# Twenty-four of the first gates' weights converted during attention in place of sixteen, with w2's conversions and three loads at other places of the order

## The chip, the core and the metric

The kernel runs on one core of one Trainium2 chip. The metric is the time of one execution on the device, in microseconds; the median of three runs of the kernel before is 1388.04 us (1387.42 to 1390.29).

## What is computed

Four batches of 12-head attention (448 positions, 64 dimensions a head) whose scores and whose probabilities are each mixed across the heads by a 12x12 matrix; then a gated feed-forward layer and a second one, over 1792 tokens of width 768:

```python
scores = einsum('bhij,hg->bgij', q @ k.T / 8, w_pre)
attn = einsum('bhij,hg->bgij', softmax(scores), w_post)
x = (attn @ v).transpose(0, 2, 1, 3).reshape(1792, 768)
x = (sigmoid(x @ w_gate) * (x @ w_val)) @ w_out          # first: 768 -> 1536 -> 768
h = x @ w_in2
out = (h * sigmoid(1.702 * h)) @ w_out2                  # second: 768 -> 2048 -> 768
```

The five feed-forward weights come as 64-bit floats. Each has to be turned into a 32-bit float on the chip, and this is the "conversion" that the change moves.

## The kernel before, in words

**Products.** Every product is made of 32-bit values split into a high and a low part, in three matmuls. A weight tile (384 columns of 128 rows) becomes a pair of parts by `high` on ScalarE (ACT, line 913) and `low` on VectorE (DVE, line 919).

**A conversion** (`convert`, lines 786 to 799) takes a piece of 384 KB from its input to a 32-bit tile of 192 KB and stores it in device memory (`kept`). It is one load on SyncE's queue (SP), two ACT instructions (lines 791, 792), three DVE instructions (lines 794, 795, 797), and a store on SP's queue (line 799). There are 136 pieces: 48 of the first layer's gate and value weights (four for each of twelve gate blocks f), 24 of its output weight, 32 of w2's input weight and 32 of w2's output weight. Sixteen of the first 48 (`self.pre`, line 633) are converted while attention runs, through one buffer `pf` for the load and two buffers `pc` for the result (`prepare`, lines 820 to 845). The other 120 are converted in the feed-forward part through buffers `ws` and `wc`.

**Attention** (lines 85 to 523) takes 180 groups of ten query rows for all heads. A group's way is: transfer of the scores (SP), split in high and low (ACT, then GpSimd or DVE, line 278), mix before (TensorE, line 285), maximum (DVE, line 292), exponential (ACT, line 299), normalizing (DVE, ACT), mix after (TensorE, line 330), copy out; and for each of 16 units of up to 12 groups the product with v (line 349). The order on each engine is made by a planner (`Work`, lines 21 to 77): each piece has a due time and costs per engine, and the planner always takes the piece that can start first, the earlier due one among equals. A conversion's pieces are due at its entry of `TIMES` (us, line 548), and its load may not be planned before that. On the chip each engine and each queue then works its own list strictly in order.

**The feed-forward part** is written out in program order. `take` (line 944) hands TensorE the next split weight, `ahead` (line 951) has four or five more weights' steps put out beyond it, `split` (line 931) puts out one step of the list `units`: pieces used at once ("f"), pieces converted and stored alone, and pieces that are made from stored ones ("o", "p", "s"). The list is written in lines 632 to 659; where a conversion stands in it sets beside which product its instructions run. In order:

- Token half t = 0, first four gate blocks ("direct", f = 0 to 3), plain products with 16 weights, each converted on the spot. Beside them `widen` (line 1232) builds sums of the activations for the faster form of product that follows: a load of x (four transfers of 224 KB) for each of three chunks, four DVE sums a chunk (line 1190), and splits. `pump` (line 1122) hands out these steps at each half product, `later_work` sets the rate.
- Four pairs of gate blocks (f = 4, 6, 8, 10), 14 products each in the faster form, whose weights are loaded back from `kept` by `lift` (line 886, four transfers of 384 KB a pair), when `allowed` and the pair's last conversion permit it. Beside the pairs run 5, 6, 5 and 3 conversions.
- The output product with 24 weights converted on the spot (line 1353); 13 conversions of w2's pieces stand between them, from the third weight on. Blocks 0 and 1 of the gates were stored, and are split again at the start (lines 1356 to 1360, so lines 983 and 985), just before they are used.
- t = 1: six pairs with three conversions each, then the output product, now with weights loaded back in twelve pairs (`kept_pair`, line 593), and two or three conversions after each, from the first on.
- Then the second layer for t = 1 and for t = 0.

Of the kernel before, what the change touches and what calls it, by code (L numbers as in the profile page):

```python
# [526 lines left out]
class Ffn:  # L527
# [16 lines left out]
    EARLY = 4  # L544
    SPILL = 2
    DIRECT = 4
    PRE = 16
    TIMES = (85, 94, 121, 124, 145, 150, 166, 190, 232, 238, 276, 292, 319, 331, 371, 382)
    NST = 5
    DOWN = 2.0 ** -112  # L550
    MOST = 122879.9921875 * DOWN
# [2 lines left out]
    def __init__(self, ctx, tc, xd, yd, gd, kept, sums2, w_gate, w_val, w_out, w2_in, w2_out, out):  # L554
# [9 lines left out]
        KG, KD, K1, K2 = self.KG, self.KD, self.K1, self.K2  # L564
# [4 lines left out]
        o1 = len(self.pieces)  # L569
# [16 lines left out]
        def whole(i, used=True):  # L586
            u = len(self.units)
            self.units.append(("f", len(self.items), i))
            self.items.append(("f", i, u + 1))
            if used:  # L590
                self.used.append(u)

        def kept_pair(i):
            u = len(self.units)
            self.used += [u, u + 1]
            self.units += [("p", len(self.items), x) for x in range(2)]
            self.items.append(("k", i, u + 3))
# [13 lines left out]
        rest = [*range(o3, len(self.pieces)), *range(o2, o3)]  # L611
        D = self.DIRECT
# [3 lines left out]
        def convert(*pieces):  # L616
            for i in pieces:
                where[i] = len(self.units)
                whole(i, False)

        def kept_own(j, others):
            loads = [[4 * (j + f) + 2 * g for f in range(2)] for g in range(2)]
            after = max(where[i + x] for y in loads for i in y for x in range(2)) + 2
            self.groups.append((loads, after))
            n = len(self.groups) - 1
            spread = [len(others) * min(x, 8) // 8 for x in range(15)]
            for x, (p, g) in enumerate((p, g) for p in self.ORDER for g in range(2)):
                self.used.append(len(self.units))
                self.units.append(("o", (n, g), p))
                convert(*others[spread[x]:spread[x + 1]])  # L630

        early = [*range(4 * D, o1)]
        self.pre = [early.pop(0) for _ in range(self.PRE)]
        where.update((i, -3) for i in self.pre)
        for i in range(4 * D):
            where[i] = len(self.units)
            whole(i)
            if early and False:
                convert(early.pop(0))
        for n, j in enumerate(range(D, K1, 2)):  # L640
            m = (5, 6, 5, 0)[n]
            convert_now = [early.pop(0) for _ in range(min(m, len(early)))]
            if j == K1 - 2:
                convert_now += [rest.pop(0) for _ in range(3)]
            kept_own(j, convert_now)
        assert not early
        for i in range(o1, o2):
            where[i] = len(self.units)
            whole(i)
            if i > o1 + 1 and (i - o1) % 5 in (0, 2, 4):  # L650
                convert(rest.pop(0))
        for j in range(0, K1, 2):
            kept_own(j, [rest.pop(0) for _ in range(3)])
        for i in range(o1, o2, 2):
            kept_pair(i)
            for _ in range(3 if i % 4 else 2):
                if rest:
                    convert(rest.pop(0))
        assert not rest
        self.ends = []  # L660
# [11 lines left out]
        self.steps = {}  # L672
        self.kblocks = []
        self.spare = 45
        self.allowed = 1
        self.later = []
        self.done = set()
        self.step = 0
# [141 lines left out]
    def prepare(self, work, pf, pc):  # L820

        last = []
        for n, i in enumerate(self.pre):
            t = self.TIMES[n] * 1e3
            tiles = {}
# [146 lines left out]
    def load(self, dst, src, c):  # L972
        self.nc.sync.dma_start(dst[:, 1].bitcast(F32), src[:, c, :])
# [258 lines left out]
    def widen(self):  # L1232

        A, X, KG = self.A, self.X, self.KG
        raw = {}

        def load(c):
            raw[c] = [self.form(F32) for _ in range(2)]
            for x, cc in zip(raw[c], (c, KG + c)):
                for h in range(2):  # L1240
                    self.nc.sync.dma_start(x[:, h], self.xd[h][:, cc, :])

        def sums(c):
            (x1, x3), (x2, x4) = ((x[:, 0], x[:, 1]) for x in raw[c])
            self.tt(x4, x3, x4, ALU.add)
            self.tt(x3, x1, x3, ALU.subtract)
            self.tt(x1, x4, x1, ALU.subtract)
            self.tt(x2, x2, x1, ALU.subtract)

        def parts(c, j):  # L1250
            for p, x in (((7, raw[c][0][:, 1]), (5, raw[c][1][:, 1])), ((6, raw[c][0][:, 0]), (3, raw[c][1][:, 0])))[j]:
                A[p].append(self.form())
                self.hilo(A[p][c], x)
            if j:
                self.after(1, lambda: self.give(*raw[c]))

        for c in range(KG):
            A[1].append(X[c][0])
            A[2].append(X[KG + c][0])
            A[4].append(X[KG + c][1])  # L1260
        yield lambda: load(0)
        yield lambda: load(1)
        for c in range(KG):
            yield lambda c=c: sums(c)
            yield lambda c=c: parts(c, 0)
            yield lambda c=c: (parts(c, 1), load(2) if c == 0 else None)
# [47 lines left out]
    def first(self, t):  # L1314

        K1, S, D = self.K1, self.S, self.DIRECT
        G = self.G = [[None, None] for _ in range(K1)]
        if t:
            self.later_work(self.sums_out(range(3), 3), 38)
        else:  # L1320
            self.A = {p: [] for p in self.ORDER}
            self.later_work(self.widen(), 4 * D - 7)
            self.spare = 12
        for f in range(K1):
            if t or f >= D:
                if f % 2:
                    self.spare = 0 if f < self.SPILL else 4
                    if f < K1 - 1:
                        self.allowed += 1
                    self.gates(t, f - 1, f == K1 - 1)  # L1330
                if t and f == 5:
                    self.rush()
            else:
                if f == 0:
                    pg, pv = (acc for acc, _ in self.going)
                else:
                    pg, pv = (self.banks(name, 2) for name in ("pg", "pv"))
                    for acc in (pg, pv):
                        for k, _ in enumerate(self.product(acc, self.X)):
                            if k % self.KG == self.KG - 1:  # L1340
                                self.pump()
                self.gated(t, f, pg, pv)
                if f == D - 1:
                    self.rush()
                    self.give(*(self.X[c][1] for c in range(self.KG)))
        self.flush()
        self.next = {p: [] for p in self.ORDER}
        if t:
            self.A = self.next
            self.later_work(self.sums_out(range(3, 4)), 17)  # L1350
        steps = K1 // self.KG
        act = G[self.KG:] + G[:self.KG]
        for m in range(self.KD):
            py = self.banks("py", 2)
            for k, _ in enumerate(self.product(py, act)):
                if m == 0 and k in (2 * self.KG - 2, 2 * self.KG - 1):
                    for h in range(2):
                        x = G[k - 2 * self.KG + 2][h]
                        self.part(self.nc.scalar, x, 0)
                        self.after(0, lambda x=x: self.part(self.nc.vector, x, 1))  # L1360
                if not t and k % self.KG == 0:
                    self.next_a(self.xd[2:], m * steps + k // self.KG,
                                {8 * c + x: [(c, i)] for c in range(self.KG) for i, x in enumerate((0, 4, 6))})
                if m == self.KD - 1:
                    self.give(*act[k])
                    if k == 0 and not t:
                        self.allowed, self.spare = self.allowed + 1, 0
                if k % self.KG == self.KG - 1:
                    self.pump()
            if t:  # L1370
                if m == 4:
                    self.rush()
                self.next_y(m, py)
            else:
                for h in range(2):
                    y = self.temp("y")
                    self.nc.scalar.copy(y, py[h][:, :S])
                    self.nc.sync.dma_start(self.yd[h][:, m, :], y)
        self.A = self.next
# [272 lines left out]
```

## Time and profile before

| | |
|---|---|
| median of three runs | 1388.04 us |
| the profiled execution | 1385.28 us |
| its span, first to last instruction | 1383.5 us |
| attention's last matmul (line 349) starts | 466.75 us |
| TensorE clock granted | 1.0 of full speed throughout |
| busy share: TensorE / DVE / ACT | 98% / 78% / 66% |

Times in all rows count from the span's start. PE is TensorE's matmuls, PEld its weight loads, POOL is GpSimd, SP is SyncE, whose work is issuing transfers. A busy time of TensorE is modelled from pipelined instructions: two back to back overlap, so the number of matmuls started in a stretch tells more than its busy share. "Idle before" is the time in which an engine stood still ahead of an instruction, with what ended it.

### The profile page before, as it was taken

What the parts mean: (1) busy time and instruction counts of PE and PEld (TensorE: products, weight loads), DVE (VectorE), ACT (ScalarE), POOL (GpSimd) and SP (SyncE); (2) the same over time, 40 slices, a digit from 0 to 9 for tenths busy, and PEclk for the clock granted to TensorE, in tenths of its full rate; (3) what the DMA queues carried; (4) which work ended last, traced back from release to release, by engine and by line L of the source; (5) the groups of instructions that cost most, each with busy time, mean ns of one, the idle gap of its engine ahead of it and who ended that gap; (6) DMA issues with size and microseconds to landing.
All of it is one profiled execution on the core that took longest, in us unless ns stands there. A gap on an engine that the chain in (4) does not pass through costs nothing.

```text
span 1383.5 us, 26030 instructions
## 1 busy us (share of the span) xinstructions
PE 1351.1 (98%) x8904; PEld 1232.7 (89%) x8904; DVE 1079.7 (78%) x2473; ACT 909.8 (66%) x2142; POOL 170.4 (12%) x160
## 2 busy tenths in 40 slices
PE   7999999999999999999999999999999999999999
PEld 5888888888888989898999999899999999999998
DVE  6788878878888879989879987887876679566664
ACT  5878778887888746767666666664766355566352
POOL 3444433433440000000000000000000000000000
PEclk9999999999999999999999999999999999999999
DMA  6645744743545675548997644687551587121574
GB/s 167 181 153 158 216 141 130 218 153 112 166 146 179 222 256 160 183 158 262 301 310 271 218 137 136 220 285 238 203 179 53 169 267 262 56 86 58 174 235 157
DMA packets 222084, 255.09 MB, mean 184 GB/s; under 512 B 70124, under 2 KB 209664, under 8 KB 221952
## 3 DMA queue, kind: packets, MB, share of 16 engines
q1 hardware_dynamic: 220928, 253.19, 56.9%
q8 instruction: 70, 1.15, 0.3%
q14 instruction: 62, 0.51, 0.1%
q10 hardware_dynamic: 960, 0.23, 0.1%
q0 software_dynamic: 64, 0.01, 0.0%
HBM read 159.92 MB, written 54.92 MB: 155 GB/s over the span
## 4 chain that ended last, share of the span: by engine, by line
PE 56%; DVE 2%; issue 1%; ACT 0%; DMA 0%; DVEq 0%; ACTq 0%
PE pq L1052 30%; PE po L1513 15%; PE py L997 11%; DVE wc L795 0%; DMA ws<-in_moe_w_in_dram 0%; DVE wc L797 0%; DVE w L919 0%; DVE xy L1034 0%; DVE wc L794 0%; DVE s L1190 0%; ACT xy L985 0%; DVE xy L983 0%; ACT wc L791 0%; DVE s L1061 0%; ACT ws L792 0%
## 5 line engine op out<-in xcount | busy, mean ns | idle before, releaser
L1052 PE MATMUL pq<-xy,w 128*128 128x448 f32 x2268 | 462.7, 365 | 1.4 <-DVE s L1190 1.3
L1052 PEld LDWEIGHTS pq<-xy,w 128*128 128x128 f32 x2268 | 425.0, 188 | 38.4 <-ACT w L913 1.7
L1513 PE MATMUL po<-wf,xy 128*128 128x384 f32 x1200 | 209.4, 336 | 0.0
L1513 PEld LDWEIGHTS po<-wf,xy 128*128 128x128 f32 x1200 | 209.1, 188 | 0.1
L278 POOL TENSOR_TENSOR ghl<-gt,ghl 120x448 fp32r<-120x448 f32 (+1 forms) x144 | 165.7, 1156 | 247.2 <-ACT ghl L214 189.8
L997 PE MATMUL py<-xy,w 128*128 128x448 f32 x864 | 177.8, 365 | 5.7 <-DVE xy L983 4.0
L330 PEld LDWEIGHTS pso<-w,ex 120*112 120x112 f32 (+1 forms) x1440 | 160.5, 177 | 24.8 <-ACT w L312 6.3
L997 PEld LDWEIGHTS py<-xy,w 128*128 128x128 f32 x864 | 161.8, 188 | 21.4 <-DVE xy L983 5.3
L330 PE MATMUL pso<-w,ex 120*112 120x120 f32 (+1 forms) x1440 | 173.3, 269 | 6.7 <-ACT ex L299 2.0
L285 PE MATMUL psp<-ghl,wphl 120*120 120x448 f32 x540 | 137.6, 383 | 2.0 <-ACT ex L299 0.9
L292 DVE TENSOR_REDUCE st<-psp 120x1 f32<-120x448 f32 x180 | 109.2, 613 | 23.1 <-PE psp L285 22.9
L299 ACT ACTIVATE ex<-psp,st 120x448 f32<-120x448 f32 x180 | 113.5, 634 | 9.1 <-DVE st L292 4.6
L1033 ACT CAST xy<-xy 128x384 fp32r<-128x384 f32 (+2 forms) x188 | 85.3, 478 | 42.3 <-DVE xy L1190 40.6
L1034 DVE TENSOR_TENSOR xy<-xy 128x384 fp32r<-128x384 f32 (+2 forms) x188 | 92.2, 509 | 19.8 <-ACT xy L1033 19.5
L285 PEld LDWEIGHTS psp<-ghl,wphl 120*120 120x120 f32 x540 | 89.1, 182 | 15.8 <-issue 2.4
L791 ACT ACTIVATE wc<-ws 128x384 f32<-128x384 f32 x120 | 66.3, 553 | 44.0 <-DMA ws<-in_moe_w_in_dram 20.1
L214 ACT CAST ghl<-gt 120x448 fp32r<-120x448 f32 (+1 forms) x141 | 79.2, 568 | 23.1 <-PE psp L285 17.0
L1190 DVE TENSOR_TENSOR xy<-xy 128x384 f32<-128x384 f32 (+1 forms) x148 | 81.5, 558 | 14.0 <-DMA xy<-xd 7.2
L919 DVE TENSOR_TENSOR w<-wt,w 128x384 fp32r<-128x384 f32 x104 | 56.9, 552 | 29.3 <-ACT w L913 29.2
L349 PEld LDWEIGHTS psv<-at,vt 112*64 112x64 f32 x1536 | 73.7, 137 | 5.4 <-issue 2.8
L349 PE MATMUL psv<-at,vt 112*64 112x120 f32 (+1 forms) x1536 | 77.1, 260 | 0.2
L913 ACT CAST w<-xy 128x384 fp32r<-128x384 f32 x100 | 50.0, 511 | 38.7 <-DVE xy L1190 34.3
(98 smaller groups left out, 1828.1 us busy)
## 6 DMA issues: line engine op xcount, KB each, us to landing
gt<-sc SPq DMA_DIRECT2D x172, 210.0 KB
wf<-sb SPq DMA_DIRECT2D x64, 384.0 KB
kept<-wc SPq DMA_DIRECT2D x120, 192.0 KB
xy<-kept SPq DMA_DIRECT2D x56, 384.0 KB
ws<-in_moe_w_out_dram SPq DMA_DIRECT2D x56, 384.0 KB
ws<-kept SPq DMA_DIRECT2D x44, 384.0 KB
sb<-xy SPq DMA_DIRECT2D x32, 384.0 KB
ws<-in_moe_w_in_dram SPq DMA_DIRECT2D x32, 384.0 KB
```

What stands on the lines that cost most here:

```text
L278: eng.tensor_tensor(out=t[:m, 1], in0=gt.pop(s)[:m], in1=t[:m, 0].bitcast(F32), op=ALU.subtract)
L285: nc.tensor.matmul(ps[:m, :S], wphl[:m, wp, :m], t[:m, gp], start=(i == 0), stop=(i == 2))
L292: nc.vector.tensor_reduce(out=st[:m, 0:1], in_=pre[s][:m, :S], axis=AX.X, op=ALU.max, negate=True)
L299: nc.scalar.activation(t[:m], pre.pop(s)[:m, :S], AF.Exp, bias=st[:m, 0:1], scale=1.0, accum_out=st[:m, 1:2])
L330: nc.tensor.matmul(ps[:JC, c, :, :n], e[:m, c * JC:(c + 1) * JC], w[:m, :, :n], start=True, stop=True)
L349: nc.tensor.matmul(ps[a * 64:a * 64 + 64, r, :n], vt[b][:, g, c, :], a_t[:, c, g, :n], start=(c == 0), stop=(c == NJ - 1), tile_position=( ...
L997: self.nc.tensor.matmul(acc[hb][:, :self.S], st, act[k0 + kc][hb][:, ap], start=(k0 + kc == 0 and part == 0 and ap == 0), stop=(k0 + kc == ...
L1033: self.nc.scalar.copy(dst[:, 0], src)
L1034: self.after(n, lambda: self.nc.vector.tensor_tensor(out=dst[:, 1], in0=src, in1=dst[:, 0].bitcast(F32), op=ALU.subtract))
L1052: nc.tensor.matmul(x, st, A[p][c][:, ap], start=(first and c + part + ap == 0), stop=(c == self.KG - 1 and part == 1), skip_group_check=no ...
L1190: self.nc.vector.tensor_tensor(out=dst, in0=x, in1=y, op=op)
L1513: nc.tensor.matmul(acc[:, :PW], x[:, part], w[:, wp], start=(start and part == 0 and wp == 0), stop=(stop and part == 1), skip_group_check ...
```

## The change

It converts 24 pieces during attention, all weights of f = 4 to 9, at other times; the other eight (f = 10, 11) are converted beside the pairs f = 4 and f = 6, four each, and four of w2's pieces each beside the pairs f = 8 and f = 10. In the first output product ten of w2's pieces are converted, from behind the sixth weight on, where there were thirteen from behind the third. In the second output product the conversions begin behind the third pair of weights, three a pair. `widen`'s first load is issued when its list is made, ahead of the first gate block's end, an empty step is put behind its second load, and the list is spread over ten hand-outs, where there were nine. The first `lift` is allowed at f = 2, and no longer from the start.

```diff
-    PRE = 16
-    TIMES = (85, 94, 121, 124, 145, 150, 166, 190, 232, 238, 276, 292, 319, 331, 371, 382)
+    PRE = 24
+    TIMES = (82, 83, 94, 128, 129, 145, 155, 159, 190, 195, 206, 229, 239, 264, 265, 278, 292, 303, 334, 335, 342, 356, 366, 391)
@@ the list of units
-            if early and False:
-                convert(early.pop(0))
         for n, j in enumerate(range(D, K1, 2)):
-            m = (5, 6, 5, 0)[n]
+            m = (4, 4, 0, 0)[n]
             convert_now = [early.pop(0) for _ in range(min(m, len(early)))]
-            if j == K1 - 2:
-                convert_now += [rest.pop(0) for _ in range(3)]
+            if j > 7:
+                convert_now += [rest.pop(0) for _ in range(4)]
             kept_own(j, convert_now)
@@
-            if i > o1 + 1 and (i - o1) % 5 in (0, 2, 4):
+            if i > o1 + 4 and (i - o1) % 2:
                 convert(rest.pop(0))
@@
             kept_pair(i)
-            for _ in range(3 if i % 4 else 2):
-                if rest:
+            for _ in range(3):
+                if rest and i > o1 + 3:
                     convert(rest.pop(0))
@@
-        self.allowed = 1
+        self.allowed = 0
@@ widen
-        yield lambda: load(0)
+        load(0)
         yield lambda: load(1)
+        yield lambda: None
@@ first
-            self.later_work(self.widen(), 4 * D - 7)
+            work = self.widen()
+            work = [next(work), *work]
+            self.later_work(work, 4 * D - 6)
@@
+                if f == D // 2:
+                    self.allowed += 1
```

## Rows read from the trace of the kernel before

**Rows 1.** The page: busy us, share of span, instructions of each engine.

```profile
PE 1351.1 (98%) x8904; PEld 1232.7 (89%) x8904; DVE 1079.7 (78%) x2473; ACT 909.8 (66%) x2142; POOL 170.4 (12%) x160
```

**Rows 2.** Chain that ended last: start us, us, what.

```profile
720.68 150.02 PE pq L1052 x738
...
874.21 5.81 DMA ws<-in_moe_w_in_dram
```

**Rows 3.** Windows: us, PE, PEld, DVE, ACT, POOL busy (count), clock, DMA share, GB/s.

```profile
476.00:524.00 48.00, 45.41 (x220) 40.74 (x219) 36.26 (x76) 25.06 (x52) 0.00 (x0) 1.00 0.74 243
...
550.00:577.00 27.00, 25.67 (x126) 23.31 (x125) 25.03 (x53) 18.51 (x40) 0.00 (x0) 1.00 0.59 190
...
629.00:660.00 31.00, 28.04 (x136) 25.11 (x135) 30.00 (x67) 23.39 (x51) 0.00 (x0) 1.00 0.93 301
...
660.00:720.00 60.00, 60.00 (x298) 55.53 (x297) 47.61 (x104) 37.53 (x82) 0.00 (x0) 1.00 0.94 312
...
872.00:890.00 18.00, 15.31 (x70) 12.44 (x68) 15.19 (x34) 10.67 (x24) 0.00 (x0) 1.00 0.73 228
...
890.00:966.00 76.00, 76.00 (x376) 70.41 (x377) 60.50 (x129) 41.62 (x92) 0.00 (x0) 1.00 0.86 284
```

**Rows 4.** Timeline of PE: start us, us, instruction, idle before.

```profile
505.98 3.10 PE L997 MATMUL pv<-xy,w 128*128 128x448 f32 x14 [1.28 <-DVE w L919]
...
557.38 71.97 PE L1052 MATMUL pq<-xy,w 128*128 128x448 f32 x351 [1.33 <-DVE s L1190]
...
643.88 16.41 PE L997 MATMUL py<-xy,w 128*128 128x448 f32 x78 [2.90 <-DVE xy L983]
...
884.23 2.75 PE L997 MATMUL py<-xy,w 128*128 128x448 f32 x11 [1.16 <-ACT xy L1033]
...
889.39 2.83 PE L997 MATMUL py<-xy,w 128*128 128x448 f32 x11 [1.14 <-DVE xy L983]
```

**Rows 5.** Timeline of SP, ACT and DVE at the first gates.

```profile
480.19 2.02 SPq L893 DMA_DIRECT2D xy<-kept  x4
...
483.25 2.81 SPq L1241 DMA_DIRECT2D xy<-xd  x4
...
489.70 0.55 ACT L791 ACTIVATE wc<-ws 128x384 f32<-128x384 f32 x1 [4.77 <-DMA ws<-in_moe_w_gate_dram]
...
492.02 2.61 DVE L1190 TENSOR_TENSOR xy<-xy 128x448 f32<-128x448 f32 x4 [7.23 <-DMA xy<-xd]
```

**Rows 6.** Groups by line, conversions and GpSimd: busy us, mean ns.

```profile
L795 DVE SCALAR_TENSOR_TENSOR pc<-pc,pf 128x384 uint32<-128x384 uint32 x16 | 11.6, 724 | 0.4
...
L797 DVE SCALAR_TENSOR_TENSOR pc<-pf,pc 128x384 uint32<-128x384 uint32 x16 | 11.0, 690 | 0.2
...
L794 DVE TENSOR_SCALAR pc<-pc 128x384 f32<-128x384 f32 x16 | 8.4, 526 | 2.9 <-ACT pc L791 2.9
...
L795 DVE SCALAR_TENSOR_TENSOR wc<-wc,ws 128x384 uint32<-128x384 uint32 x120 | 66.1, 551 | 0.8
...
L797 DVE SCALAR_TENSOR_TENSOR wc<-ws,wc 128x384 uint32<-128x384 uint32 x120 | 66.4, 554 | 1.8
...
L794 DVE TENSOR_SCALAR wc<-wc 128x384 f32<-128x384 f32 x120 | 42.4, 353 | 22.0 <-ACT wc L791 21.8
...
L278 POOL TENSOR_TENSOR ghl<-gt,ghl 120x448 fp32r<-120x448 f32 (+1 forms) x144 | 165.7, 1156 | 247.2 <-ACT ghl L214 189.8 <-DVE st L292 14.6 <-DVE ghl L214 8.3
```

**Rows 7.** Windows in attention, as in rows 3; the last: tile pc alone.

```profile
40.00:440.00 400.00, 391.56 (x3799) 341.50 (x3798) 326.96 (x881) 325.28 (x852) 157.56 (x137) 1.00 0.51 160
...
340.00:360.00 20.00, 20.00 (x192) 17.09 (x189) 16.62 (x40) 14.88 (x37) 6.30 (x6) 1.00 0.41 142
...
340.00:360.00 20.00, 3.41 (x6) 0.88 (x2) 1.00 0.41 142
```

**Rows 8.** Tiles pc, sc: ns min/median/max, first and last start.

```profile
L799 SPq DMA_DIRECT2D kept<-pc x16: 331/345/607, 110.3 to 409.4; - x16
...
L214 DVE COPY sc<-psq x97: 596/610/625, 10.6 to 426.3; 120x448 f32<-120x448 f32 x70, 88x448 f32<-88x448 f32 x27
```

## The prediction, made before the change was run

> **What bounds the kernel now.** I read the page first. TensorE is busy 98% of the span, DVE 78% [rows 1]; so whatever the change does to DVE, ACT or transfers counts only where TensorE stands still for it. The chain of waits comes next: in the feed-forward part it runs through TensorE for long unbroken pieces (738 matmuls in 150.02 us, 0.203 us each) and leaves it in a few short places, as where a load of w2 holds it for 5.81 us [rows 2]. The windows by stage then say what these places cost. An undisturbed stretch starts 298 matmuls in 60 us, 0.2013 us each [rows 3]. Against that:
>
> - 476 to 524 (direct gate blocks): 220 started where 238 fit; 18 x 0.2013 = 3.6 us lost.
> - 550 to 577 (pair f = 6): 126 where 27 / 0.203 = 133 fit; 1.4 us.
> - 629 to 660 (output product, t = 0): 136 where 154 fit; 3.6 us.
> - 872 to 890 (output product, t = 1): 70 where 89 fit; 3.9 us [rows 2, 3].
>
> Together 12.5 us, and the timeline of TensorE shows an idle row in each place, with a late DVE or ACT instruction as its end [rows 4]. Attention is another kind of stage: TensorE is busy 391.56 of 400 us there, while DVE has 73.0 and ACT 74.7 us idle [rows 7]. The change takes work out of the four places and puts it into that stage.
>
> **Direct blocks: widen's first load earlier, the first lift later.** Now SP issues the lift (four transfers of 384 KB) at 480.19 and only then, at 483.25, the first load of x; the DVE sums that need it stand at the head of DVE's list and wait 7.23 us, and the weights that TensorE then waits for are queued behind them [rows 4, 5]. With the load ahead of the first block's end it is issued some 5 us sooner (the 2.02 us of the lift, the wait for the gate, and a hand-out), and 1.5 MB of the lift no longer travels with it. The sums keep their hand-out, the third. So I count the 7.23 us wait as gone and with it the stalls: 3.2 of 3.6 us, between 1.28 (the longest idle row alone) and 3.6. What it passes: on SP the load now stands before the two stores of the first gate, which is 2.81 us of issue [rows 5]; they free two of seven buffers, which nobody wants for a whole gate block of about 14 us. The lift, at f = 2, puts four issues (2.02 us) before weight loads; that is a rival below. It has until the first pair at 524, some 30 us. The empty step moves the second chunk's sums back by one hand-out; I cost it and the tenth hand-out at nothing, since the splits are forced out before the first pair anyhow.
>
> **Pairs: 5, 6, 5, 3 conversions become 4, 4, 4, 4.** A conversion takes DVE 0.353 + 0.551 + 0.554 = 1.46 us [rows 6]. In pair f = 6 DVE is busy 25.03 of 27 us and the stall ends on a DVE sum [rows 3, 4]; two conversions less are 2.9 us less. I take all 1.4 us (bounds 0 and 1.4). The last pair gets one conversion more, early in the pair; DVE's idle time there covers it, and if it did not, up to 1.46 us would come back in the next item.
>
> **First output product.** DVE is busy 30.00 of 31 us, and TensorE waits 2.90 us for the low parts of the stored gate blocks, which stand in DVE's list behind the conversions [rows 3, 4]. By the new list two of w2's conversions that were ahead of them come later: 2 x 1.46 = 2.9 us. I take 2.9 of the 3.6 us (0 to 3.6). Later on ten conversions stand where thirteen did.
>
> **Second output product.** Here the list opened with w2 conversions whose loads had not landed; ACT works in order and waited for them, and the last gates' splits and the stored blocks' splits came late: idle rows of 1.16 and 1.14 us [rows 2, 4]. No conversion now stands beside the first two pairs of weights, five fewer. I take 3.7 of 3.9 us (0 to 3.9). The price lies behind it: three conversions a pair of weights where 2.5 were. From 890 to 966 the DMA share is 0.86 [rows 3]; it rises to at most 0.86 x 3 / 2.5 = 1.03, less as far as it is other traffic. I take nothing for it, since 660 to 720 ran at 0.94 and lost none [rows 3]; the upper bound is 0.03 x 76 = 2.3 us.
>
> **Attention: eight more conversions.** In this stretch the three DVE instructions take 0.526 + 0.724 + 0.690 = 1.94 us, a third more than the same instructions in the feed-forward part; what is there and not here is GpSimd, 1.156 us an instruction [rows 6]. Eight are 15.5 us of DVE's 73.0 idle; ACT's two instructions and the transfers (share 0.51) have more room [rows 7]. The cost for TensorE is not in any row. Below: nothing, as the stretch from 340 to 360 holds the work of two conversions (six DVE instructions, 3.41 us) and TensorE was busy all of it [rows 7]. Above: all 15.5 us. In between: TensorE's 8.4 idle us of the 400 come from late work on engines that are 82% busy; if they grow as DVE's ratio of busy to idle time does, from 327/73 to 342.5/57.5, that is a factor of 1.33, 2.8 us more. Nearest are the window without loss and this estimate; I take 2.0. A gain is not excluded either, as all pieces get another order: as much the other way, 2.8. On SP each new load waits for the one buffer `pf`, with the score transfers of later groups behind it; these are planned four groups ahead, which covers a few us.
>
> By the Trainium skill (SBUF — State Buffer, "Who interferes with whom") a DVE instruction with two SBUF inputs, or in a two-port mode, and a GpSimd instruction that reads SBUF hold one shared port by turns, and the later one is blocked until the other has ended. The longer durations agree with it. By that rule alone the added 24 DVE instructions could each wait out one of GpSimd's, 24 x 1.156 = 27.7 us of DVE, where the rows of the present conversions make it 8 x 0.48 = 3.9; this estimate is no end of my range.
>
> **Sum.** 3.2 + 1.4 + 2.9 + 3.7 = 11.2 us gained, 2.0 paid: 9.2 us. The profiled execution took 1385.28 us (span 1383.5), 2.8 under the median of three, 1388.04; so 1376.1 for a like execution and **1378.8** for the median. A measurement of this kernel can tell about 0.2%, 2.8 us, from no change.
>
> **Rivals.**
>
> *DVE in attention becomes the bound (slower).* The place is DVE's in-order list: each conversion holds a maximum or a copy behind it, whose group's whole chain waits. If all 1.94 us of each is paid, +15.5 - 11.2 = +4.3: 1392.3. It decides from 1.4 us a conversion on. For it: those stretched durations [rows 6]. Against: the unhurt window and 73 us of idle DVE [rows 7]. The skill's port rule above is its mechanism. Chance 0.09.
>
> *DMA fills up in the second output product.* The start is freed, but three conversions a pair of weights outrun the transfers: 2.3 us back, 9.2 - 2.3 = 6.9: 1381.1; if late loads also bring the 3.7 us back, 1384.8. For it the bound of 1.03, against it the 0.94 without loss. Chance 0.17.
>
> *The lift is now in the weights' way.* Its 1.5 MB at f = 2 delay weight loads as they did at 480, where ACT waited 4.77 us for one [rows 5]. Then the direct blocks stall as before: 9.2 - 3.2 = 6.0, 1382.0. Against it: weights are made four ahead, some 14 us. Chance 0.10.
>
> *The conversions end too late: no change.* The last store of a conversion came at 409.4, 27.4 us behind its time of 382, and the feed-forward part may open only after both it and the last scores at 426.3 [rows 8]. With 391 it is 418.4. With 24 in one buffer the lag may grow; past 35 us every further us delays the first weights, and 9 us more would take the gain: 1388. Chance 0.08.
>
> **How the numbers follow.** The forecast's own case has 0.56. Its own range: from all 12.5 with no cost in attention (1375.5), or 2.8 gained there (1372.7), to the low bound of the direct blocks and the last pair's 1.46 paid, 9.2 - 1.92 - 1.46 = 5.8 (1382.2). The range of 8 in 10 goes on to the middle cases and stops short of the slow one: 1372.5 to 1387. Faster by over 0.2% (under 1385.3) holds nearly all of the first case and of the two middle ones, a little of the late end: 0.78. Within 0.2%: the late end, and the edges of the others: 0.13. Slower (above 1390.8): the DVE case, 0.09.
>
> **What would show it.** Right: the idle row of the sums on DVE (7.23) gone; 236 or more matmuls in the 48 us of the direct blocks; no idle row on TensorE in pair f = 6; the row of 2.90 under 1; none over 0.5 at the second output product; attention's last product with v starting within 3 us of 466.75. Wrong: that start later by 10 or more; conversions in attention far over 1.94 us on DVE; a DMA share near 1 with idle rows of TensorE behind 890; or the four stalls still there, each behind another instruction.

## The result, and the profile after

| | before | after |
|---|---|---|
| median (lowest to highest) of 6 runs | 1388.80 us (1386.96 to 1390.60) | 1377.09 us (1375.46 to 1377.82) |
| profiled execution / its span | 1385.28 / 1383.5 us | 1377.82 / 1375.9 us |
| attention's last matmul starts | 466.75 us | 470.48 us |
| from there to the end of the span | 916.7 us | 905.4 us |

The ratio is 0.9914, with a 95% interval of 0.9903 to 0.9925: 11.7 us faster by the medians. The compared profiles differ by 7.5 us only; the last section says where the rest comes from.

The windows of after by stage, which answer to [rows 3, 7]: us, PE, PEld, DVE, ACT, POOL busy (count), granted clock, DMA share, GB/s.

```profile
476.00:524.00 48.00, 48.00 (x238) 44.48 (x238) 39.77 (x82) 29.88 (x62) 0.00 (x0) 1.00 0.86 291
550.00:577.00 27.00, 27.00 (x134) 24.82 (x133) 23.73 (x50) 17.78 (x38) 0.00 (x0) 1.00 0.49 156
627.00:658.00 31.00, 29.86 (x146) 27.04 (x146) 29.69 (x65) 22.90 (x50) 0.00 (x0) 1.00 0.89 281
658.00:718.00 60.00, 60.00 (x298) 55.52 (x297) 47.41 (x104) 36.31 (x78) 0.00 (x0) 1.00 0.91 304
869.00:887.00 18.00, 18.00 (x90) 16.64 (x90) 15.94 (x36) 12.65 (x27) 0.00 (x0) 1.00 0.73 243
887.00:958.00 71.00, 71.00 (x353) 65.74 (x352) 56.16 (x121) 39.95 (x87) 0.00 (x0) 1.00 0.86 283
...
40.00:440.00 400.00, 391.48 (x3788) 338.56 (x3789) 332.82 (x890) 334.88 (x869) 161.76 (x139) 1.00 0.56 171
```

Three of the four places run as fast as undisturbed stretches: 238 matmuls in 48 us where 220 stood, 134 where 126, 90 where 70. The first output product has 146 where 136 were. The DMA share behind the second product's start is 0.86 and nothing is lost there.

The timeline of TensorE in after says the same (start us, us, instruction, idle before). A row without an idle entry is one unbroken run.

```profile
516.96 7.46 PE L995 MATMUL pv<-xy,w 128*128 128x448 f32 x36
524.26 103.14 PE L1050 MATMUL pq<-xy,w 128*128 128x448 f32 x504
627.24 11.52 PE L995 MATMUL py<-xy,w 128*128 128x448 f32 x56
639.83 76.80 PE L995 MATMUL py<-xy,w 128*128 128x448 f32 x376 [1.08 <-DVE xy L981]
...
774.23 96.80 PE L1050 MATMUL pq<-xy,w 128*128 128x448 f32 x475 [0.44 <-DVE w L917]
870.88 87.68 PE L995 MATMUL py<-xy,w 128*128 128x448 f32 x432
```

Of the stalls of [rows 4], 1.28, 1.33, 1.16 and 1.14 are gone, 2.90 is 1.08, and a small new one of 0.44 stands among the six pairs of t = 1. On SP and DVE at the first gates of after, the load of x (line 1239) stands ahead of the stores of the gates, and the sums (line 1188) no longer wait:

```profile
480.36 2.87 SPq L1239 DMA_DIRECT2D xy<-xd  x4
483.33 0.85 SPq L1024 DMA_DIRECT2D gd<-sg  x2
...
488.27 2.59 DVE L1188 TENSOR_TENSOR xy<-xy 128x448 f32<-128x448 f32 x4
```

The row of 7.23 us idle [rows 5] has no successor.

### The profile page after: what moved, and what is told of

Read it like the earlier page. It is cut to its first block, busy times and chain, and to the rows that moved or that the text cites. A ratio compares the mean times of both kernels' runs of the same rounds, so it can differ in the third digit from the quotient of the medians.

```text
span 1375.9 us, 26033 instructions
## 1 busy us (share of the span) xinstructions
PE 1350.6 (98%) x8904; PEld 1231.9 (90%) x8904; DVE 1076.8 (78%) x2465; ACT 915.1 (67%) x2149; POOL 174.2 (13%) x161
## 4 chain that ended last, share of the span: by engine, by line
PE 71%; DVE 7%; DMA 3%; ACT 2%; issue 2%; POOL 0%; SPq 0%; DVEq 0%; ACTq 0%; POOLq 0%
PE pq L1050 29%; PE po L1516 15%; PE py L995 12%; PE pso L330 4%; PE psv L349 3%; PE psp L285 2%; PE pg L995 2%; PE pv L995 2%; PE psq L245 1%; DMA sb<-xy 1%; DVE st L292 1%; DMA xy<-kept 1%; DMA gt<-sc 1%; ACT ex L299 1%; DVE w L917 1%
## 5 line engine op out<-in xcount | busy, mean ns | idle before, releaser
L278 POOL TENSOR_TENSOR ghl<-gt,ghl 120x448 fp32r<-120x448 f32 (+1 forms) x145 | 169.5, 1175 | 245.9 <-ACT ghl L214 193.7
L285 PE MATMUL psp<-ghl,wphl 120*120 120x448 f32 x540 | 141.8, 386 | 4.9 <-POOL ghl L278 1.7
L789 ACT ACTIVATE wc<-ws 128x384 f32<-128x384 f32 x112 | 62.0, 554 | 39.3 <-DMA ws<-in_moe_w_in_dram 20.6
L214 ACT CAST ghl<-gt 120x448 fp32r<-120x448 f32 (+1 forms) x137 | 76.3, 569 | 16.5 <-PE psp L285 9.8
L312 ACT ACTIVATE w<-wpost,st 120x120 f32<-120x120 f32 x180 | 69.9, 399 | 9.5 <-DVE st L309 8.0
```

The costliest lines, as they stand in the source:

```text
L278: eng.tensor_tensor(out=t[:m, 1], in0=gt.pop(s)[:m], in1=t[:m, 0].bitcast(F32), op=ALU.subtract)
L285: nc.tensor.matmul(ps[:m, :S], wphl[:m, wp, :m], t[:m, gp], start=(i == 0), stop=(i == 2))
```

## The experiments

Stages tell more than totals here. A stage runs from the start of its first matmul to the start of the next stage's first, read from TensorE's timeline. Attention's entry is the start of its last matmul with v; the 24 matmuls of the first gate block that run before it are not counted to the direct blocks. All in us, one profiled execution each; the stages not shown differ by about 1 at most, but for one start of the second layer, of which the text tells.

| kernel | attention | direct | 4 pairs | 1st output | 6 pairs | 2nd output |
|---|---|---|---|---|---|---|
| before | 466.75 | 57.32 | 104.94 | 91.34 | 153.68 | 91.77 |
| before_again | 466.46 | 56.76 | 105.00 | 92.90 | 155.34 | 94.60 |
| after | 470.48 | 53.61 | 102.97 | 89.24 | 154.40 | 87.51 |
| after_again | 468.86 | 53.61 | 102.90 | 89.24 | 153.68 | 87.51 |
| att_only | 470.74 | 57.39 | 103.22 | 92.97 | 153.92 | 92.46 |
| no_dve_in_attention | 467.23 | 53.61 | 102.98 | 89.24 | 153.68 | 87.52 |
| times_shifted | 468.43 | 53.61 | 102.91 | 89.24 | 153.68 | 87.51 |
| loads_only | 464.91 | 53.61 | 104.41 | 92.42 | 153.52 | 94.24 |
| load_first_lift_as_before | 468.26 | 53.61 | 104.58 | 92.86 | 153.52 | 93.04 |
| second_output_only | 466.26 | 57.36 | 104.95 | 92.53 | 153.94 | 89.09 |
| first_output_later | 468.62 | 57.46 | 104.95 | 89.24 | 154.72 | 92.71 |
| second_output_28 | 466.08 | 56.77 | 104.97 | 92.93 | 153.99 | 87.48 |
| sixteen_in_attention | 467.69 | 53.61 | 106.09 | 89.18 | 155.90 | 87.52 |
| parts_first | 469.89 | 53.61 | 102.91 | 87.56 | 154.18 | 87.52 |

The theory was the prediction's: four separate stalls go, attention pays about 2 us. Its rivals were that attention pays more through DVE, that the lift gets in the way, and that one part does most of the work.

### The kernel before once more (before_again, no edit)

> The kernel before, unchanged, for a second profile. If attention's length varies from run to run, as the medians suggest (11.7 us between them, where the two profiles lie 7.5 us apart), the last matmul with v starts somewhere from 466 to 471 us and the part behind it again takes 916.7 us, within 0.5. If attention is as fixed as the rest, it starts at 466.75 within 0.5, and the profiled execution takes 1385 us.

Its profiled execution took 1390.71 us (span 1388.9); 15 timed runs of before beside it have a median of 1388.83. The two profiles of one program differ by 5.4 us, nearly all of it from the first output product to the second: 92.90, 155.34 and 94.60 us in place of 91.34, 153.68 and 91.77. So neither of the two expected cases came: attention was as long as before, but the part behind it took 922.4 us where it took 916.7. In the first output product the idle row is as long as before and only the granted clock differs; in the second the clock differs and the idle rows are 0.9 us longer; in the six pairs three small idle rows, 0.9 us together, are new at a full clock. The last section has the clock.

### Attention's part alone

```diff
 (on before)
-    PRE = 16
+    PRE = 24
-    TIMES = (85, 94, ...
+    TIMES = (82, 83, 94, ...
```

> The kernel before with PRE and TIMES of the change alone: eight conversions more in attention, which leaves 5, 3, 0 and 3 beside the four pairs. Theory (attention covers them): the part behind the last matmul with v falls by the 2.0 us that the pairs gave, from 916.7 to some 914.7; attention takes 0 to 4 us more than that of the kernel before, so the time is between 2 us faster and 2 us slower. Rival (DVE's list in attention becomes the path): 8 x 1.94 = 15.5 us more in attention, 13.5 us slower in all.

1391.05 us against 1388.83 of before: ratio 1.0016 (1.0005 to 1.0027). Attention's end moves from some 466.9 us (mean of the eight profiles with the old order, 464.9 to 468.6) to 470.74; with after and after_again (468.86) the mean of the new order is 470.0. So the eight conversions cost attention about 3.1 us. Profiles of one order differ by as much among themselves, so this mean is an estimate, uncertain by 1 to 2 us. What their going buys is the pair stall alone (103.22). The part behind attention takes 918.4 us and not the expected 914.7: both stalls in the output products stay, and the clock falls behind each, as in before_again (922.4) and unlike the first profile of before (916.7). By itself this part loses.

### Attention's DVE work left out

```diff
 (on after, prepare)
-            for j, engines in enumerate((dict(ACT=(920, 1140)), dict(DVE=(270, 360)), ...
+            for j, engines in ((0, dict(ACT=(920, 1140))), (4, dict(SP=(700, 3000)))):
```

> The changed kernel with the three DVE instructions of all 24 conversions in attention left out (loads, ACT's two and the stores stay; the weights stored are not the weights), 24 x 1.96 = 47 us of DVE. Theory (hidden): attention is at most 3 us shorter, the rest unchanged, time within 0.25% of the changed kernel's. Rival (DVE's list is the path there, a third of the work or more on it): 16 us or more faster.

1373.26 us, 0.9885 (0.9863 to 0.9907) of before; that is 3.8 us under after, 0.28% where at most 0.25% was expected. Loads, ACT's step and stores of all 24 stay. Taking away all 47 us of DVE work (24 x 1.957, from the groups below) moves attention's end from 470.0 to 467.2, 2.8 us, by one profile of this kernel; the planner also orders the rest anew when these pieces are gone. The groups of after in attention by line (busy us, mean ns of one | idle before), which answer to [rows 6], and one of them by tile (ns min/median/max):

```profile
L278 POOL TENSOR_TENSOR ghl<-gt,ghl 120x448 fp32r<-120x448 f32 (+1 forms) x145 | 169.5, 1175 | 245.9 <-ACT ghl L214 193.7 <-PE psq L245 13.5 <-PE pso L330 12.7
...
L793 DVE SCALAR_TENSOR_TENSOR pc<-pc,pf 128x384 uint32<-128x384 uint32 x24 | 18.6, 775 | 0.8
L795 DVE SCALAR_TENSOR_TENSOR pc<-pf,pc 128x384 uint32<-128x384 uint32 x24 | 16.0, 666 | 0.2
...
L792 DVE TENSOR_SCALAR pc<-pc 128x384 f32<-128x384 f32 x24 | 12.4, 515 | 5.1 <-ACT pc L789 5.1
...
L793 DVE SCALAR_TENSOR_TENSOR pc<-pc,pf x24: 540/558/1466, 95.7 to 420.9; 128x384 uint32<-128x384 uint32 x24
```

The three DVE instructions have 775 + 666 + 515 = 1.96 us, where the sixteen had 1.94. Half of them run as fast as in the feed-forward part (median 558 ns); a few of up to 1466 make the mean. DVE is not attention's bound: by these profiles some 6% of the conversions' DVE work reaches TensorE (an estimate, 2.8 of 47 us).

### The conversions due at other moments

```diff
 (on after)
-    TIMES = (82, 83, 94, 128, ...  356, 366, 391)
+    TIMES = (86, 87, 98, 132, ...  360, 370, 387)
```

> The changed kernel with every entry of TIMES 4 us later (the last 4 earlier): the same work in another order of attention. If attention's length depends on the order that the planner happens to find, it moves by 1 us or more, either way; if on the work alone, it stays within 0.5 us of the changed kernel's (by the medians). The part behind it takes 905.5 us within 0.5.

1376.43 us (1375.36 to 1378.91), which can't be told from after's 1377.09. Attention ends at 468.43, where the other moments gave 468.86 to 470.74. Of the two expected cases neither is shown: the shift is no larger than the 1.6 us between two profiles of the unchanged kernel. The last store's moment sets nothing either. By tiles in after, the last store of a conversion starts 8 us before the last copy of the scores [rows 8]:

```profile
L797 SPq DMA_DIRECT2D kept<-pc x24: 330/344/489, 97.7 to 422.1; - x24
...
L214 DVE COPY sc<-psq x100: 594/609/625, 10.1 to 430.1; 120x448 f32<-120x448 f32 x75, 88x448 f32<-88x448 f32 x25
```

### The loads alone, and without the later lift

```diff
 (on before)
-        self.allowed = 1
+        self.allowed = 0
...
-        yield lambda: load(0)
+        load(0)
         yield lambda: load(1)
+        yield lambda: None
...
-            self.later_work(self.widen(), 4 * D - 7)
+            work = self.widen()
+            work = [next(work), *work]
+            self.later_work(work, 4 * D - 6)
...
+                if f == D // 2:
+                    self.allowed += 1
```

The second kernel leaves out the two edits of `allowed`.

> The kernel before with the edits of the loads alone (widen's first load ahead, the empty step, ten hand-outs, the first lift at f = 2). Theory: the wait of DVE for x was what delayed the weights, so the direct blocks take 53.6 us where they took 57.3 and nothing else changes: 3.7 us less behind attention. Rival (the lift's transfers delay the weights anyway): 55 us or more, with TensorE waiting behind loads of the gates' weights.

> As loads_only, but the first lift stays allowed from the start, so its four transfers follow widen's first load on the queue, ahead of the weights. If the early load alone cures the stall, the direct blocks take 53.6 us as there; if the 1.5 MB of the lift still hold up x or the weights, 54.5 to 57.

1383.77 us, 0.9964 (0.9951 to 0.9977), and 1385.27 us, 0.9981 (0.9965 to 0.9997), against 1388.17 of before. The direct blocks take 53.61 us in both. The earlier load of x alone does it; the lift's place changes nothing there, and its 1.5 MB at f = 2 harm nothing. In the profiles all of the difference between the two lies in attention (464.91 and 468.26), which the lift doesn't touch; behind it the second is even 1.0 us shorter (915.2 for 916.2). A part of the difference is the clock: in the second kernel's profile TensorE stands idle for 2.23 us at 24.5, and from 28 to 32 the granted clock is 0.62, where it is 1.00 in loads_only. The other stalls stay, as the timeline of TensorE in loads_only shows:

```profile
551.36 71.91 PE L1052 MATMUL pq<-xy,w 128*128 128x448 f32 x351 [1.33 <-DVE s L1190]
...
637.79 77.89 PE L997 MATMUL py<-xy,w 128*128 128x448 f32 x376 [2.88 <-DVE xy L983]
...
879.93 2.75 PE L997 MATMUL py<-xy,w 128*128 128x448 f32 x11 [2.01 <-ACT xy L1033]
...
885.10 78.34 PE L997 MATMUL py<-xy,w 128*128 128x448 f32 x376 [1.16 <-DVE xy L983]
```

### The second output product's list alone, with 30 conversions and with 28

```diff
 (on before)
-            for _ in range(3 if i % 4 else 2):
-                if rest:
+            for _ in range(3):
+                if rest and i > o1 + 3:
 (second_output_28 also)
-                convert_now += [rest.pop(0) for _ in range(3)]
+                convert_now += [rest.pop(0) for _ in range(5)]
```

> The kernel before with the rule of the second output product alone: no conversion beside the first two pairs of weights, three beside each later one. Theory: the first weights no longer wait behind conversions whose loads are late, so that product takes 87.5 us where it took 91.8, 4.3 us less, nothing else. Rival (the transfers fill up): 88.5 us or more, with the DMA share near 1 and TensorE idle at some later weight.

> The kernel before with the rule of the second output product (as in second_output_only) and two of w2's conversions more beside the last pair of the first half, five for three, so that 28 and not 30 are left for the second product. Theory (two conversions too many at its end were what stopped the second layer's start): the second output product takes 87.5 to 89 us, the first stretch of the second layer 102.6 where second_output_only had 106.2; time 3 to 5 us below the kernel before. Rival (three a pair of weights fill the transfers whatever their number): that stretch stays over 104.5, no gain.

The first: 1388.52 us, 1.0000 (0.9987 to 1.0013). Its product runs without a stall (87.64 us for 432 matmuls), but the stalls come back behind it. TensorE's timeline in second_output_only, and one row of DVE's:

```profile
875.22 87.64 PE L997 MATMUL py<-xy,w 128*128 128x448 f32 x432
964.31 0.67 PE L1052 MATMUL pq<-xy,w 128*128 128x448 f32 x2 [1.45 <-ACT w L913]
966.11 4.94 PE L1052 MATMUL pq<-xy,w 128*128 128x448 f32 x23 [1.12 <-DVE w L919]
971.77 19.39 PE L1052 MATMUL pq<-xy,w 128*128 128x448 f32 x94 [0.73 <-DVE xy L1034]
991.97 8.28 PE L1052 MATMUL pq<-xy,w 128*128 128x448 f32 x39 [0.81 <-DVE w L919]
...
960.17 0.56 DVE L855 TENSOR_TENSOR wt<-ws 128x384 f32<-128x384 f32 x1 [4.03 <-DMA ws<-kept]
```

With the rule alone 30 pieces are left for ten pairs of weights, three behind every pair to the last, and the loads of the second layer's first weights come late: DVE stood still 4.03 us for one. The idle rows make 4.1 us, and the second layer's first stage takes 106.2 us where it took 102.6 in before. The transfers are behind there: their share is 0.90 from 880 to 940, and they still run from 960 to 965 (0.85), when the product ends. That is the mechanism of the prediction's rival of full transfers, felt one stage later than the prediction put it.

With two pieces given to the pair f = 10 before, 28 are left, as in after, and the time is 1382.29 us, 0.9954 (0.9939 to 0.9969), 6.3 us under the 1388.59 beside it. The second output product takes 87.48 us and the second layer's first stage 103.10; the transfers are done by 960 (a share of 0.00 from 960 to 965), before the product ends at 962.4. So this part of the change is worth its price only with the two pieces moved elsewhere.

### The first output product's list alone

```diff
 (on before)
-            if i > o1 + 1 and (i - o1) % 5 in (0, 2, 4):
+            if i > o1 + 4 and (i - o1) % 3:
```

> The kernel before with the same thirteen conversions of w2 in the first output product, but none before the sixth weight. Theory (two conversions of DVE stood ahead of the stored blocks' low parts): that product takes 88.9 to 89.5 us where it took 91.3; about 1 us of the stall stays. Rival (DVE is late there from the pairs on): 90.5 or more.

The number of conversions in it stays at 13. The stage does as expected: 89.24 us, as in after. The total doesn't show it: 1387.54 us, 1.0001 (0.9988 to 1.0014), with ten runs from 1385.6 to 1393.4. The product is 3.7 us shorter than in before_again, and the medians show 0.6. In the profile attention ended at 468.62 and the six pairs took 154.72, both above most others; whether the later conversions cause that or whether it is spread isn't settled.

### All but the eight conversions in attention

```diff
 (on after)
-    PRE = 24
+    PRE = 16
-    TIMES = (82, 83, 94, ...
+    TIMES = (85, 94, ...
-            m = (4, 4, 0, 0)[n]
+            m = (5, 6, 5, 0)[n]
-            if j > 7:
-                convert_now += [rest.pop(0) for _ in range(4)]
+            if j > 9:
+                convert_now += [rest.pop(0) for _ in range(6)]
-            if i > o1 + 4 and (i - o1) % 2:
+            if i > o1 + 4 and ((i - o1) % 2 or i - o1 in (10, 16)):
```

> The changed kernel with sixteen conversions in attention as before, and the eight others back beside the pairs: 5, 6, 5 and 6 conversions there, twelve (from behind the sixth weight on) in the first output product, 28 in the second; loads as changed. Theory: attention is 3 to 4 us shorter than in the changed kernel, the pairs take 1.5 to 3 us more and the first output product 1 to 3 us more; in all from 1 us faster to 2 us slower than the changed kernel, 0.9905 to 0.993 of the kernel before. Rival (the eight must leave the pairs for the rest to work): stalls return in the pairs and the output products, 0.996 or more.

1377.58 us, 0.9923 (0.9908 to 0.9938), beside 1376.31 of after_again. All four runs of it (from 1376.66) lie above all four of after_again (to 1376.53), but by so little that a difference is suggested and not shown. Twenty-two conversions beside the pairs cost two stalls there (timeline of TensorE):

```profile
554.14 51.82 PE L1050 MATMUL pq<-xy,w 128*128 128x448 f32 x252 [1.33 <-DVE s L1188]
607.32 20.41 PE L1050 MATMUL pq<-xy,w 128*128 128x448 f32 x99 [1.36 <-DVE s L1188]
```

That is 106.09 us for 102.90 in the pairs, and two idle rows of 0.77 and 0.75 stand in the six pairs (155.90 for 153.68); attention gives back 1.2 to 2.8. Here the profile shows more than the median: the profiled execution, 1380.19 us, is the slowest of the four. Against what was expected, the first output product is no longer than in after (89.18), and attention gains less than 3 to 4 us. The eight conversions in attention are a trade of nearly equal terms, worth 1.3 us by the medians. Most of the gain of the change comes from its other parts.

### The stored blocks split first

```diff
 (on after, with the TIMES of times_shifted)
-                if m == 0 and k in (2 * self.KG - 2, 2 * self.KG - 1):
+                if m == 0 and k < 2:
                     for h in range(2):
-                        x = G[k - 2 * self.KG + 2][h]
+                        x = G[k][h]
```

> The changed kernel with the shifted TIMES and with the stored gate blocks split at the first two steps of the output product, ahead of the conversions that delayed them in DVE's list. Theory: the stall of 1.1 us that is left there goes, the first output product takes 87.5 us where it took 89.2, and attention ends as in times_shifted, 2 us before the changed kernel's; time 1373 to 1375, 0.989 to 0.990 of the kernel before. Rival (another weight is late instead, as conversions now wait behind the splits): 89 us there, no gain over times_shifted.

1373.76 us (1373.56 to 1375.01), 0.9894 (0.9880 to 0.9909) of before, 2.6 under after_again (1375.43 to 1376.53) on the same chip. Of this the stage accounts for 1.7 us, 87.56 for 89.24; the rest isn't placed, for attention ended at 469.89, and not where it did in times_shifted. The low parts of the two stored blocks (line 981) are put out with the first two of the product's twelve blocks, no longer with the fifth and sixth, and so stand ahead of some of the weights' conversions in DVE's list; they are used at the tenth and eleventh. The first output product in its timeline is one row:

```profile
626.57 87.72 PE L995 MATMUL py<-xy,w 128*128 128x448 f32 x432
```

### The kernel after once more (after_again, no edit)

> The changed kernel, unchanged, on the same chip as parts_first and sixteen_in_attention, for their comparison. Theory: 1376 to 1378.5; attention's last matmul with v starts at 470 to 471, the part behind it takes 905.5 within 0.5, the clock is granted in full throughout, as no idle time of TensorE over 1.3 us is left in the feed-forward part.

1376.31 us (1375.43 to 1376.53), 0.9911 (0.9895 to 0.9928); its profile has the span 1373.5. Attention ends at 468.86, 1.6 us before the first profile of the same kernel and below the expected 470 to 471; the part behind it takes 904.6, below the 905.5 within 0.5. The 0.44 of the first profile in the six pairs of t = 1 is absent, 153.68 us. The clock is granted in full throughout, as expected.

## Why the prediction was right

It said 1378.8 us, in a range of 1372.5 to 1387, with 0.78 for faster; 1377.09 was measured. By its own terms, against the two compared profiles:

| term | predicted | measured |
|---|---|---|
| direct blocks | -3.2 | 57.32 to 53.61, -3.7 |
| pairs | -1.4 | 104.94 to 102.97, -2.0 |
| first output product | -2.9 | 91.34 to 89.24, -2.1 |
| second output product | -3.7 | 91.77 to 87.51, -4.3 |
| all the rest behind attention | 0 | +0.8 |
| attention | +2.0 | +3.7; by means of several profiles +3.1 |
| sum | -9.2 | -7.5; with +3.1, -8.1 |

The second profile of after gives +2.1 for attention and -9.9 for the sum: what one profile says of attention is uncertain by the size of the term. Two of the signs that the prediction named for being right failed narrowly in the compared profile: attention's last matmul with v starts 3.7 us later and not within 3, and the row of 2.90 is 1.08 and not under 1.

- **Direct blocks.** The mechanism held: the earlier load, and not the lift, took the wait away. Counted from attention's last matmul, the load is issued 6.6 us sooner, where some 5 were predicted. All of the 3.6 us lost came back; the price for the stores moved back on SP and the empty step was nothing, as costed. The rival that the lift gets in the weights' way is false here.
- **Pairs.** The stall in pair f = 6 is gone with four conversions there in place of six. With three there and the rest of before left as it was it is gone too (att_only, 103.22); with twenty-two beside the four pairs two stalls come back.
- **First output product.** The term was too large by 0.8. Moving two conversions left one late row of 1.08, for the low parts still stand behind the weights' own conversions. parts_first shows it: 87.56 us, 1.7 less.
- **Second output product.** All came back, and the rival of full transfers did not arise in the whole change: the share stays at 0.86 against the bound of 1.03. What the prediction had not seen is how near the edge this was. It priced the denser conversions by the product's own window, while at 30 pieces the price falls due in the next stage, 3.6 us in second_output_only; the edits to the pairs' list, which it had priced for DVE alone, are what takes the two pieces out.
- **Attention.** The least certain term: 2.0 against 3.1 by the means, and 3.7 and 2.1 by the two profiles of after. The in-between estimate of 2.8 lies nearer to the mean, but the spread between profiles of one order doesn't exclude 2.0. The window without loss [rows 7] was one of many, and no single window showed this cost: 40 to 440 us of after has TensorE as busy (391.48) as before (391.56), though 11 matmuls fewer start in it.
- **DVE as attention's bound.** Rejected by no_dve_in_attention. By the Trainium skill (SBUF — State Buffer, "Who interferes with whom") a DVE instruction with two SBUF inputs and a GpSimd instruction that reads SBUF exclude each other on a shared port. The trace agrees in kind: the means of 775 and 666 ns stand against 550 and 553 in the feed-forward part, where GpSimd rests; but no run took GpSimd's work away, so that it is the cause isn't shown. The trace does not agree with the extreme that the prediction worked out from it, 27.7 us for 24 more instructions: 24 conversions together lost (1.957 - 1.456) x 24 = 12.0 us on DVE, most of it hidden.
- **Conversions that end too late.** They ended 8 us before the scores, as the tiles show.
- **From profile to median.** This step failed. The prediction took the 2.8 us between the profile of before and its median as a constant offset of the kernel and added it to the forecast. After has none: 1377.82 in its profile, 1377.09 in its median. By the medians the gain is 7.5 + (1388.80 - 1385.28) + (1377.82 - 1377.09) = 11.7. What the offset probably was is told in the last section. That it made up for the terms of attention and of the first output product, and so brought 1377.09 near to 1378.8, is luck.

The parts don't add up one by one: by the differences of medians att_only +2.2, loads_only -4.4, second_output_only +0.4 and first_output_later -0.6 make -2.4, all together -11.7. With second_output_28 (-6.3) in place of second_output_only they make -9.1, so most of the gap is the two pieces that have to go elsewhere; the rest is not assigned. Each conversion has to stand somewhere, and a list thinned at one place alone thickens another.

## What to carry to other kernels

Price an edit to an in-order list at the place where the moved instructions end up as well as where they leave; a stall that disappears at the head of a list is often standing behind its end, and a part that is worth nothing alone may be worth its whole price once another part makes room. Move work to an engine's idle time only for what it buys at the other end: here the eight conversions in attention cost about as much as they gained, and the order of a few splits was worth more. Where the median lies well off the profile, look for what differs between executions before carrying the difference over.

## What the runs showed of the chip that was not expected

A stall of some 2 to 3 us in dense matmuls mostly cost more than itself. The profile that the prediction read has a granted clock of 1.00 throughout; in before_again the clock falls behind each of the two large stalls. Windows of before_again (columns as above; the granted clock is the third number from the end), then its timeline of TensorE:

```profile
641.00:644.00 3.00, 0.84 (x3) 0.55 (x4) 2.95 (x7) 1.42 (x5) 0.00 (x0) 1.00 1.06 382
644.40:647.60 3.20, 3.20 (x10) 2.82 (x10) 3.20 (x9) 1.53 (x4) 0.00 (x0) 0.51 1.00 336
648.00:651.00 3.00, 3.00 (x17) 2.78 (x16) 1.22 (x3) 2.68 (x7) 0.00 (x0) 1.00 0.70 263
884.00:888.00 4.00, 1.50 (x8) 1.04 (x6) 3.43 (x8) 0.94 (x2) 0.00 (x0) 1.00 0.79 230
890.00:896.00 6.00, 5.13 (x14) 3.64 (x13) 5.97 (x14) 4.41 (x11) 0.00 (x0) 0.50 0.86 281
...
643.09 78.36 PE L997 MATMUL py<-xy,w 128*128 128x448 f32 x376 [2.88 <-DVE xy L983]
...
888.12 4.35 PE L997 MATMUL py<-xy,w 128*128 128x448 f32 x13 [2.62 <-ACT xy L1033]
```

After 2.88 us of idle the clock is at 0.51, the level of 1.2 GHz, for about 3.4 us and then at 1.00, 2.4 GHz, again: 10 matmuls start in 3.20 us, and 17 in the 3.00 us from 648. Behind the second stall, 2.62 us and soon after 0.87 more, it is at 0.50 from 890 to about 896.6. The 376 matmuls behind the last stall of each product took 78.36 and 78.04 us where they took 76.81 and 76.74 in the first profile of before, 2.9 us more together. In att_only a stall of 1.84 us is followed by 0.50 from 890 to 893, too. Behind the rows of 1.28 to 1.36 us in the direct blocks and the pairs the clock stays at 1.00 in every profile. Kernels in which one stall is gone lose the clock behind the other only. In second_output_28, whose stall at the first output product stayed, and in first_output_later, where that one is down to 1.08 us and the second product's stayed, the windows behind the two places are:

```profile
642.50:646.00 3.50, 3.24 (x10) 2.69 (x11) 3.50 (x9) 2.37 (x5) 0.00 (x0) 0.73 1.05 375
887.00:890.00 3.00, 3.00 (x17) 2.77 (x16) 2.63 (x6) 1.32 (x4) 0.00 (x0) 1.00 1.06 393
```

```profile
643.00:646.00 3.00, 2.14 (x9) 1.75 (x10) 3.00 (x8) 1.51 (x4) 0.00 (x0) 1.00 0.92 293
886.50:890.00 3.50, 3.50 (x12) 3.04 (x12) 3.09 (x8) 3.50 (x10) 0.00 (x0) 0.58 0.82 288
```

None of the six profiles whose idle rows in the output products are 1.1 us or less (after, after_again, times_shifted, no_dve_in_attention, sixteen_in_attention, parts_first) has such a drop there. In the 47 timed runs of before beside the experiments the mean granted clock of the span is 0.993 to 1.000: 14 runs at 0.996 have a mean of 1388.7 us, 12 at 0.998 one of 1387.8, the one at 1.000 took 1384.8. In after's six runs it is 0.999 or 1.000. So the profile read for the prediction, 1385.28 us, was an execution without the drop, and the median, some 3 us above it, very likely stands for executions with it. That the change also won these 3 us by removing the stalls is argued from these numbers; no run changed the clock alone. Why the clock fell in most executions of before and not in that one, behind stalls of the same length (2.90 and 2.88 us), stays open, and so does what in attention's new order costs its 2 to 4 us.
